# A hand-written issue order of 1190 steps is replaced by another: attention and wave-MLP on one core

## The chip, the cores and the metric

The kernel runs on one core of a Trainium2 chip. The metric is the device time of one execution in microseconds (us), as the median of several runs. The kernel before takes 230.06 us (three runs, 229.84 to 230.63).

The core has a matrix engine TensorE (PE, with its weight load PEld shown apart), VectorE (DVE), ScalarE (ACT), GpSimd (POOL), and SyncE (SP), which here only issues DMAs. PE writes into PSUM, which has eight banks of 128 x 512 float32; the other engines read PSUM and write SBUF.

## The reference

There are two parts, one after the other, for 8 batches of 576 positions:

```python
# attention: q, k, v are (8, 8, 576, 64); factor 4, scale 1/8
q_d, k_d, v_d = means of q, k, v over groups of 4 positions        # 144 positions
out_d  = softmax(scale * q_d @ k_d.T) @ v_d                         # pooled
out_up = np.repeat(out_d, 4, axis=2)
scores = np.where(np.abs(i - j) < 4, scale * q @ k.T, -1e9)         # local band
x = out_up + softmax(scores) @ v                                    # then (8, 576, 512)
# wave-MLP
theta = x @ w_theta
y = einsum('ts,bsd->btd', w_tok_r, x * cos(theta)) + einsum('ts,bsd->btd', w_tok_i, x * sin(theta))
u = x + y
return u + np.maximum(u @ w_ch, 0.0)
```

Inputs and output are float32; the kernel computes in bfloat16 with float32 sums.

## The kernel before

The whole kernel is one list of steps. The string `ORDER` (from L57) holds 1190 words. A word is a kind of step in two letters and a place of one or two characters; the loop at L758 takes the words from left to right and issues the next step of that kind. Steps of one kind come in a fixed sequence (batch by batch, the table `STEPS` at L720), so a word says when the next one comes, not which. The place is, for casts, copies and products, the engine (`a` ACT, `v` DVE, `g` POOL); for steps that write PSUM, one bank or two (`23` is banks 2 and 3); for loads, one of 16 staging slots in SBUF in base 36 (`NSTG`, L44). A function `pin` (L744) ties every instruction to the one issued before it on its engine, so the words set the order on each of the five engines exactly. Between engines only data, banks, buffers and slots make one wait for another.

One batch passes through these kinds:

- Loads on SP: `lk`, `lq` (L287, 288 KB each, four for a batch, two heads each), `lv`, `lw` (L347, two halves of a v tile, 128 KB); weights once: `la` (theta, L240), `lb` (W_tok, nine loads, L253 to L257), `lc` (channel, L240). v of batch 0 comes whole (`l1`, L365). A slot is free again when its cast has read it.
- Casts to bfloat16: `ck`, `cq` (L295, tiles k_tm, q_tm), `cv` (L396), `ca`, `cc` (L243), `cb` (L261).
- `tp` transposes q and k on PE (L302, nine 128x128 matmuls, two banks), `ev` copies the result to kT or qT (L315). For batch 7 a DMA transposes (`dk`, L306) and L312 copies.
- `kd`, `qd`: sums over four positions (on POOL in two products, L329 and L332 or L335; on DVE L321); `pv`, `vd`: those of v (L404, L407; L412).
- Pooled attention: `sd` scores (L426), `ed` exponentials on ACT (L437, tile pd), `nd` product with vd (L447, L452), `xn` division, `xd`, `xc` transposition (L466, L470).
- Local attention in windows of 64: `ps` scores (L482, three units a batch), `ex` exponentials on ACT (L490, tile pm), `mk` the band mask (L503 on POOL, L505), `po` product with v (L515, five chunks), `nm` division on DVE (L523, L524, tile tmp), `xt` transposition (L537), `xa` adds both parts into xT (L545, DVE).
- Wave-MLP: `th` theta (L556, four matmuls of 512 columns, four steps a batch), `cs` cosine and sine on ACT (L561, L562), `tt`, `ct`, `zt`, `zp`, `zc` or the DMA `dz` (L568, L573, L574, L577, L587, L590, L581) the same for the last 64 positions; `xm` transposes x (L595, on PE; for batches 6 and 7 the DMA `dx`, L605), `zz` multiplies (L620, DVE); `mx` mixes the tokens (L636, nine matmuls of 288 columns, eight steps a batch), `ua` adds x (L641, DVE, tile uT).
- Output: `up` and `uc` transpose u on PE (L650, L653) for batches 0 to 3, the DMA `du` (L645) for 4 to 7; `ch` the channel product (L666, four matmuls), `rl` ReLU and sum on DVE (L674, tile osb), `st` the store (L680). `ut`, `dt`, `ht`, `rt`, `ss`, `sr` do the last 64 positions for two batches at a time (L656, L695, L700, L709).
- `wp`, `wc`: W_tok is transposed on PE once (L273) and copied to WT (L278), nine steps, between the first batches.
- `te`, `ts`: an Exp or a Sin of one column on ACT (L770), put ahead so that the table of that function is loaded before it is needed; the compiler puts an ACT_TABLE_LOAD wherever the function's set changes. `wm`: matmuls on zeros (L764), that keep PE at work while the first loads come.

Batches overlap: while the wave-MLP of one is on PE, the scores of the next two are.

The loop itself:

```python
    for word in ORDER.split():
        kind, place = word[:2], word[2:]
...
        if kind in TABLE:

            nc.scalar.activation(out=idle, in_=pihc, func=TABLE[kind])
            pin()
            continue
        STEPS[kind][0](*next(todo[kind]), place)
        pin()
```

Of the kernel before, what the change touches and what calls it, by code (L numbers as in the profile page):

```python
# [57 lines left out]
kcg l10 l11 l12 l13 kcv lk4 lq5 c1a wm7e0 kcg c1g t101 lk6 lk7 ckg c1a ckg c1v t123 e1a kcv e1v wm737 tp01 x12 cqa x13  # L58
lq8 x14 cka x15 cqg evv cva lk9 tp67 ckg cvv cva lqa lqb tp01 lk1 cqg x14 cva wm521 evv evv cqa qdv tp23 cva la3 eva
pv47 vda wm624 ps01 kdg la6 ps23 ex kdv ckg lq4 ex wm656 wm717 lq2 ps01 qdg lk5 sd67 mkv ckv cqg sd45 po23 ed lk8 cag  # L60
ed ex po67 lq9 lba nm cba nd45 nm nd23 xn cag mkg cqa tp01 po67 xn po45 nm lkb eva xd0 mkg ckg lq7 cka xca la1 po23 nm
# [1 line left out]
evv lw th0 th2 lv0 cbv lw zz cbg tt3 xm4 lv3 cs cbg cbv ct cbg cbg cs lvb lw lw wp0 wcv wp1 wcv ztg wp5 th3 wp1 lv8
wcv xm2 cbg xm0 zz zp7 tp45 cs qdg wp3 wp6 zz wcv lw zz wcv wcv zca eva wp7 wcv wp1 wca te wp0 wcv ps34 ps56 ex ex
ps12 mx0 lq1 cvg lk2 lka mx7 lqc mx3 qdv cvg ua lk7 ex ua lk0 mkv mkv kdg sd67 po45 nm sd12 lq4 cva lk5 lk9 cvg cvg ed
ed mx0 ua ua lq3 pv67 po45 po23 nm mx0 vda mkg nd67 lk8 nd45 lkb nm xn xn lq6 ckg ckg tp12 mx3 po45 ua lca ua nm cqg
cqg tp67 eva eva xd0 ckg ckg up1 lq7 po23 lvc xcv nm tp45 xt67 cqg mx0 cqg xt23 eva xt45 lv4 qdg kdg uca lw lv0 lw lw
lv3 lv1 lw lw xa xa tp67 cka ts ckg ckg th1 th2 xa th5 lk8 xm4 evv cs cqg xm1 ckv th3 zz tt4 up6 lq6 lqb cs zz tp12
xm7 ua cs ucv ct cs cqg eva te ztv xm6 zz zz mx0 ua tp34 zp7 tp56 ps12 zcv mx7 mx0 ex cvv kdg evv eva lk7 lk9 cvg lk4
qdg ua up7 uca sd12 mkv ps34 po56 ex ua ccv lcc lc5 kdg nm mkv mx0 sd34 ed po56 cvg cvg ua cqg mx7 nm ua ed mx0 ua lk2  # L70
cka cqg ps67 lqd lq0 cva po45 nm lca ex po23 ckg ckg nm pv01 lvb mx6 vda lk6 utv lw tp45 eva lv1 lw cca ccv nd01 nd23
ua xn xn qdg tp67 mx5 eva lv8 lv9 cqg cqg lw lw ccg ps34 qdg ps67 ua ps12 kdv ex ex xd0 lva xca lw mkg mkg lqc lq0 ch5
rl ckg ckg cvg cvg ch3 sd67 xt45 mkg ed rl ex ts mx0 xa xt67 po45 lv5 th1 cs xa nm ua tp23 th7 up4 up1 ucv xt56 xa mkv
lv4 ch0 eva po56 po23 cvg lq2 tt4 uca th1 cs th7 nm st nm xm2 lqb rl lq1 zz lqd ct cvg xm6 lw cqg ch5 cs zz cs cqa te
up0 up1 rl sd23 ucv po67 ch4 nm rl ch0 rl ucv tp67 lv7 ed cvg pv45 vdv lk8 lk9 eva st st tp23 eva xm0 ztg lk0 lka lw
xm1 zz zz zp7 ch6 zca lvc lv3 kdg nd45 xn nd23 ckg tp01 cva xn qdg utg mx7 cka ps23 rl kdg eva ps01 ua po45 mx6 up7 ex
ex lw lw lv8 nm qdg lw cqg po45 cqg ucv lvb lv2 lw sd23 sd01 lv5 ed mx7 lw lw ua tp23 nm xd4 ed ckg ckg xca st evv
# [730 lines left out]
```

## Time and profile before

| | |
|---|---|
| median of 3 runs | 230.06 us (229.84 to 230.63) |
| span of the profiled execution, first to last instruction | 232.2 us |
| instructions | 9404 |
| PE busy (PEld) | 217.7 us (152.6) |
| DVE, ACT, POOL busy | 187.7, 156.2, 145.0 us |
| mean granted clock of PE | 0.993 |
| share of the 16 DMA engines, main queue | 81.9% |
| read from and written to HBM | 33.98 and 9.44 MB |

The profile is of one execution, whose span is 2.1 us above the median of the timed runs. Its times run from the first instruction. A row of a view names the line of the kernel, the engine, the operation, output and input tiles, and in brackets the idle time of the engine ahead of it with what ended that. A busy PE is one whose matmuls follow each other; matmuls are pipelined, so a row's duration can overlap that of the next.

### The profile page before, as it was taken

What the parts mean: (1) busy time and instruction counts of PE and PEld (TensorE: products, weight loads), DVE (VectorE), ACT (ScalarE), POOL (GpSimd) and SP (SyncE); (2) the same over time, 40 slices, a digit from 0 to 9 for tenths busy, and PEclk for the clock granted to TensorE, in tenths of its full rate; (3) what the DMA queues carried; (4) which work ended last, traced back from release to release, by engine and by line L of the source; (5) the groups of instructions that cost most, each with busy time, mean ns of one, the idle gap of its engine ahead of it and who ended that gap; (6) DMA issues with size and microseconds to landing.
All of it is one profiled execution on the core that took longest, in us unless ns stands there. A gap on an engine that the chain in (4) does not pass through costs nothing.

```text
span 232.2 us, 9404 instructions
## 1 busy us (share of the span) xinstructions
PE 217.7 (94%) x3943; PEld 152.6 (66%) x3970; DVE 187.7 (81%) x367; ACT 156.2 (67%) x243; POOL 145.0 (62%) x192
## 2 busy tenths in 40 slices
...
GB/s 217 395 390 390 291 114 238 361 300 118 265 391 179 165 245 285 243 142 214 205 165 347 307 213 115 206 153 92 67 149 109 71 127 193 138 159 137 142 227 245
DMA packets 76795, 49.41 MB, mean 213 GB/s; under 512 B 61136, under 2 KB 61392, under 8 KB 76752
## 3 DMA queue, kind: packets, MB, share of 16 engines
q1 hardware_dynamic: 76096, 47.76, 81.9%
q10 hardware_dynamic: 656, 1.05, 1.3%
...
HBM read 33.98 MB, written 9.44 MB: 187 GB/s over the span
## 4 chain that ended last, share of the span: by engine, by line
PE 60%; DMA 10%; POOL 10%; issue 6%; ACT 5%; DVE 4%; SPq 4%; DVEq 0%; POOLq 0%; ACTq 0%
PE PS L636 21%; PE PS L666 9%; PE PS L556 8%; DMA st<-in_q_dram 6%; PE PS L302 4%; POOL two L329 3%; PE PS L515 2%; SPq L347 2%; DMA st<-in_k_dram 2%; PE PS L537 2%; DMA ur<-uT 2%; POOL q_tm L295 2%; PE PS L482 2%; PE PS L447 1%; PE PS L595 1%
## 5 line engine op out<-in xcount | busy, mean ns | idle before, releaser
L636 PE MATMUL PS<-WT,z 128*128 128x288 bf16 x576 | 78.0, 287 | 0.0
L636 PEld LDWEIGHTS <-z 128*128 128x128 bf16 x576 | 53.9, 98 | 15.9 <-issue 1.3
L641 DVE TENSOR_TENSOR uT<-PS,xT 128x288 bf16<-128x288 f32 x64 | 28.6, 452 | 12.7 <-PE PS L636 10.9
L561 ACT ACTIVATE cs<-PS,pihc 128x512 bf16<-128x512 f32 x32 | 22.0, 689 | 21.1 <-PE PS L556 13.4
L556 PE MATMUL PS<-wth,xT 128*128 128x512 bf16 x116 | 30.8, 383 | 0.7 <-issue 0.2
L666 PE MATMUL PS<-wch,uT 128*128 128x512 bf16 (+1 forms) x122 | 29.8, 373 | 0.9 <-issue 0.6
L524 DVE TENSOR_TENSOR tmp<-PS,rl 128x512 bf16<-128x512 f32 x40 | 27.7, 692 | 1.4
L545 DVE TENSOR_TENSOR xT<-PS,xdT 128x928 bf16<-128x928 f32 (+1 forms) x24 | 22.3, 952 | 3.7 <-PE PS L537 2.3
L674 DVE SCALAR_TENSOR_TENSOR osb<-PS,ur 128x512 f32<-128x512 f32 x28 | 19.1, 687 | 7.1 <-DMA ur<-uT 3.0
L490 ACT ACTIVATE pm<-PS 128x1024 bf16<-128x1024 f32 (+1 forms) x24 | 20.5, 880 | 6.2 <-PE PS L482 6.1
L577 POOL TENSOR_TENSOR zT<-xT,cst 128x512 bf16<-128x512 bf16 x7 | 9.7, 1383 | 20.6 <-ACT cst L574 20.6
L295 POOL CAST k_tm<-st 128x576 bf16<-128x576 f32 x23 | 15.1, 668 | 11.2 <-DMA st<-in_k_dram 11.1
L396 POOL CAST v_w<-st 128x512 bf16<-128x512 f32 x21 | 13.3, 651 | 10.6 <-DMA st<-in_v_dram 10.5
L770 ACT ACT_TABLE_LOAD x15 | 19.2, 1283 | 0.3
L666 PEld LDWEIGHTS <-uT 128*128 128x128 bf16 x132 | 11.9, 98 | 11.2
L562 ACT ACTIVATE cs<-PS 128x512 bf16<-128x512 f32 x32 | 19.1, 597 | 0.0
L556 PEld LDWEIGHTS <-xT 128*128 128x128 bf16 x128 | 11.7, 99 | 10.6 <-issue 0.6
L295 POOL CAST q_tm<-st 128x576 bf16<-128x576 f32 x23 | 15.4, 686 | 4.9 <-DMA st<-in_q_dram 4.7
L503 POOL TENSOR_TENSOR pm<-pm,band 128x512 bf16<-128x512 bf16 x16 | 18.3, 1164 | 0.0
L329 POOL TENSOR_TENSOR two<-qT 128x576 f32<-128x576 bf16 x14 | 16.5, 1177 | 0.7 <-ACT qT L315 0.4
L620 DVE TENSOR_TENSOR z<-PS,cs 128x1024 bf16<-128x1024 bf16 x24 | 15.8, 684 | 0.5 <-ACT cs L562 0.3
L437 ACT ACTIVATE pd<-PS 128x864 bf16<-128x864 f32 x16 | 13.8, 889 | 2.5 <-PE PS L426 2.5
...
## 6 DMA issues: line engine op xcount, KB each, us to landing
...
```

The costliest lines, as they stand in the source:

```text
L295: COPY[w](out=to, in_=of)
L329: nc.gpsimd.tensor_tensor(out=t, in0=src[:, :, 0:2], in1=src[:, :, 2:4], op=ALU.add)
L490: nc.scalar.activation(out=pm[(3 * b + u) % NPM][:, :, 0:n].rearrange("p e c j w -> p e (c j w)"), in_=at.pop(("ps", b, u))[:, :, 0:4 * W ...
L524: nc.vector.tensor_tensor(out=tmp[(NCH * b + c) % NTMP].rearrange("p g (j d) -> p g j d", d=D), in0=ps[:, :, :, 0:D], in1=r.unsqueeze(3).t ...
L545: nc.vector.tensor_tensor(out=xT[b % 2][:, :, lo:lo + cnt].rearrange("p e (m j) -> p e m j", j=4), in0=at.pop(("xt", b, u))[:, :, 0:cnt].r ...
L556: nc.tensor.matmul(out=ps, lhsT=xT[b % 2][:, dc, P * c:P * c + P], rhs=wth[:, dc, :], start=(dc == 0), stop=(dc == 3))
L561: nc.scalar.activation(out=t[:, 0, :], in_=ps, func=AF.Sin, bias=pihc, scale=1.0)
L562: nc.scalar.activation(out=t[:, 1, :], in_=ps, func=AF.Sin, bias=0.0, scale=1.0)
L636: nc.tensor.matmul(out=ps, lhsT=z[b % 2][:, j, P * dc:P * dc + P], rhs=WT[:, j, cols], start=(j == 0), stop=(j == 8))
L641: nc.vector.tensor_tensor(out=uT[b % 2][:, dc, cols], in0=at.pop(("mx", b, i)), in1=xT[b % 2][:, dc, cols], op=ALU.add)
L666: nc.tensor.matmul(out=ps[:, cols], lhsT=uT[b % 2][:, dc, P * c:P * c + P], rhs=wch[:, dc, cols], start=(dc == 0), stop=(dc == 3))
L770: nc.scalar.activation(out=idle, in_=pihc, func=TABLE[kind])
```

## The change

Only the string `ORDER` changes; no line of code does, nor how many steps of each kind there are. Seen per step, 820 of the 1190 stand in another place of their engine's order, 95 casts, copies, means and products have another engine, and many have other banks or slots. The engines of the places sum up as (before, after): `ck` POOL 23, 20, ACT 7, 9; `cv` POOL 21, 18, ACT 13, 17; `uc` ACT 9, 4, DVE 7, 12; `zt` POOL 7, 5; `cb` ACT 1, 3, POOL 6, 6, DVE 2, 0; `kd`, `qd`, `mk`, `ev`, `cq`, `xc`, `zc`, `cc`, `ut`, `c1` by one to three. The warm-up matmuls at the very start have other banks, and one word `wm010` adds one of 64 columns. The hints `te` and `ts` stand at other places, and in five places more the function's set changes: 21 table loads in place of 16.

Lines of the order around the mask of batch 6 (`sd56 mkv po23` before, `mkv ex sd23 xt01 ed th7 ch5 xa po23` after), and those of the sines of batch 0:

```diff
-up0 uca th4 lvb sd56 mkv po23 lw lw xt01 utg dt ua dk7 cvv nm th7 du ed ts evg nd56 xa nd23 tt0 xn xn ct qdg mkv mkg
-tp67 cag xt45 la0 xt01 nm lb3 lb4 lb5 cqg lbc xa lba lb2 xt23 xa eva tp67 lb8 cqg lb1 caa ts th4 kdg cs cbg xm5 xa lv7
...
+lkc lbd lbe lbf lb0 lq5 xt45 eva cba cag cbg cba nm xa eva lb6 lq2 lv1 ckg lva lbd kdg cag xt67 cbg cbg lw lbb lw tp23
+xa xt01 cba ts th4 cs th6 xm7 cbg cqg evv th5 xa cs tt0 ct wp4 cqv zz wp6 cs wcv th1 wcv ztv xm0 wp6 zz wp7 zp5 wcv
...
+mx5 ex up4 ua mkv ex sd23 xt01 ed th7 ch5 xa po23 th6 nd01 nm tt2 ch3 xn nd01 lv0 st evg dkb mkg lv1 ss st st lve lw
```

ACT ahead of the sines of batch 0. The names: uT are the halves that hold W_tok here, q_tm and k_tm casts of batch 1, kT and qT their transposed copies, xdT the pooled part of x, cs cosine and sine. Before:

```order
L261 CAST uT_111<-st 128x576
L295 CAST q_tm_79<-st 128x9x64
L315 COPY kT_63<-PS 128x2x576
L295 CAST k_tm_74<-st 128x9x64
L470 COPY xdT_99<-PS 128x576
L315 COPY qT_65<-PS 128x1152
L243 CAST wth<-st 128x512
L770 ACT_TABLE_LOAD
L770 ACTIVATE idle<-pihc 128x1
L561 ACTIVATE cs_105<-PS,pihc 128x512
```

After:

```order
L243 CAST wth<-st 128x512
L295 CAST q_tm_79<-st 128x9x64
L295 CAST k_tm_74<-st 128x9x64
L315 COPY kT_63<-PS 128x2x576
L261 CAST uT_111<-st 128x576 x2
L315 COPY qT_65<-PS 128x1152
L261 CAST uT_112<-st 128x576
L770 ACT_TABLE_LOAD
L770 ACTIVATE idle<-pihc 128x1
L561 ACTIVATE cs_105<-PS,pihc 128x512
```

Two more casts of W_tok (L261) stand ahead of the table load, and the copy L470 is gone from ACT; the cast of W_theta (L243) comes first instead of last.

SP around the loads of batches 5 and 6. Before; the two k loads of the row after the ten v loads are of batches 6 and 7, and the eight q loads behind them are all of batch 6's and 7's:

```order
L680 DMA out_dram<-osb_122 128x512
L680 DMA out_dram<-osb_118 128x512
L680 DMA out_dram<-osb_119 128x512
L695 DMA_TRANSPOSE utr<-ut_115 128x4x128
L347 DMA st<-in_v_dram 64x8x64 x10
L287 DMA st<-in_k_dram 128x576 x2
L287 DMA st<-in_q_dram 128x576 x8
L347 DMA st<-in_v_dram 64x8x64
L287 DMA st<-in_k_dram 128x576
```

After; here the q load alone in the third row is batch 6's first, and the next two its second and third:

```order
L287 DMA st<-in_k_dram 128x576
L347 DMA st<-in_v_dram 64x8x64 x3
L287 DMA st<-in_q_dram 128x576
L347 DMA st<-in_v_dram 64x8x64 x3
L287 DMA st<-in_q_dram 128x576 x2
L347 DMA st<-in_v_dram 64x8x64
L680 DMA out_dram<-osb_121 128x512
L287 DMA st<-in_k_dram 128x576 x2
L347 DMA st<-in_v_dram 64x8x64 x2
L287 DMA st<-in_q_dram 128x576
L347 DMA st<-in_v_dram 64x8x64
```

The q loads of batch 6 come among those of k and v of batches 5 and 6 and ahead of three stores (L680) that stood before them.

SP around the transposes of u of batch 4 (ur0<-uT0). z1<-zT is the last part of z of batch 5, osb are stores. Before:

```order
L645 DMA_TRANSPOSE ur0_113<-uT0_111 128x4x128
L680 DMA out_0_dram<-osb4_122 128x512
L581 DMA_TRANSPOSE z1_104<-zT_110 128x4x128
L347 DMA st_126<-in_v_dram 64x8x64 x2
L645 DMA_TRANSPOSE ur0_113<-uT0_111 128x4x128 x2
L347 DMA st_126<-in_v_dram 64x8x64
L680 DMA out_0_dram<-osb0_118 128x512
```

After:

```order
L645 DMA_TRANSPOSE ur0_113<-uT0_111 128x4x128
L680 DMA out_0_dram<-osb3_121 128x512
L709 DMA out_0_dram<-osb2_120 64x512
L680 DMA out_0_dram<-osb4_122 128x512
L645 DMA_TRANSPOSE ur0_113<-uT0_111 128x4x128
L347 DMA st_126<-in_v_dram 64x8x64
L645 DMA_TRANSPOSE ur0_113<-uT0_111 128x4x128 x2
L581 DMA_TRANSPOSE z1_104<-zT_110 128x4x128
```

The last two transposes of ur0, which stood behind z1 and two v loads, now stand ahead of z1, and one v load stands between them and the one before.

More of the change, by code (lines that the diff above doesn't have):

```diff
@@ L57 @@
 ORDER = """
[L58 to L61, printed above, removed]
-tp67 cag xt45 la0 xt01 nm lb3 lb4 lb5 cqg lbc xa lba lb2 xt23 xa eva tp67 lb8 cqg lb1 caa ts th4 kdg cs cbg xm5 xa lv7
@@ L63 @@
[L63 to L77, printed above, removed]
@@ L78 @@
-tp01 eva mx6 mkg xt45 xt23 ua ua cva cvg cvg xt01 cka ts cvg xa xa mx7 th6 xa po45 nm pv23 tt0 th1 lk4 xm4 st st mkg
-th5 vdv st cs nd23 ua zz ct cqg cqg ztg tp67 th4 cs dt po01 cs cs te xn evv po23 mx5 kdg qdg xm4 xm6 mx7 nm ps01 ex nm
-ps23 ua lvd ua ex ch5 ps01 ex qdg zz lw lw xm7 zz rl kdg zp6 zz mkg nd23 xn lv1 lva lv3 mx5 zca sd67 lw ps01 ex po34
-mx2 ua lw ed tp01 sd67 cva nm po34 eva cvv cvg ed lw up5 uca ua mx2 cvg nm cvg lvc xd3 ua pv04 xcv lk7 lk0 mx7 lq9 lq6
-lq2 lqd lq8 lqb lq5 ckg ckg vda lq7 lw xt56 mkv cqg cqg po34 lk4 xt01 xa xa ch2 st cva ts lv6 th5 up6 ckg xm0 nm th1
@@ L93 @@
[L93 to L96 removed]
+wm0e0 l10 c1v l11 lk2 c1g l13 l14 lk5 t101 lq6 lk7 lq8 lq9 c1g cka kcg c1v ckg kcv t123 lk0 e1a tp45 cqg kcg cqg cqg
@@ new lines @@
+wm637 kcv e1v x10 eva cka x13 x12 cvv x14 tp56 cka cva cvv evv lq1 x17 tp01 evv cva cqg cva tp23 la2 lv3 lk5 wm521 lq6
+la4 laa pv67 wm524 eva kdg ps23 lb7 lk0 lq1 lk9 lb8 vda ps01 qdv kdv ps45 wm656 wm617 ex qdg cqg ckg sd23 ex mkv po01
+sd67 ed ckv ed po23 ex nm caa cqa wm010 nm mkg nd67 nd45 xn po23 po01 cka mkg cag xn tp67 xd4 nm nm xcv po23 tp01 lab
+lkc lbd lbe lbf lb0 lq5 xt45 eva cba cag cbg cba nm xa eva lb6 lq2 lv1 ckg lva lbd kdg cag xt67 cbg cbg lw lbb lw tp23
+xa xt01 cba ts th4 cs th6 xm7 cbg cqg evv th5 xa cs tt0 ct wp4 cqv zz wp6 cs wcv th1 wcv ztv xm0 wp6 zz wp7 zp5 wcv
@@ new lines @@
+up6 th7 ucv xt01 up6 ch5 xa cva uca po01 po23 tt4 th6 rl ckv cs cqa nm xm7 th5 ct zz ch4 xm7 nm cqg mkg ckg mkg cvg
+ckg cs up6 rl cs zz sd23 uca po01 ckg ztg cvg qdg cqg up4 ch5 nm ch6 tp01 ucv rl ed rl pv45 lv6 tp23 lw lq3 lkd lw eva
+xm6 zp7 lw lv1 lk2 lw st vdv xm0 lv5 lv0 lq9 lkc ch1 zca zz zz eva nd45 nd67 tp23 xn ps45 xn rl eva ex mx0 ua ps23
+po67 up4 kdg qdg mx5 ckg cqa ex uca nm sd01 po23 ua sd67 mx4 nm ed xd5 cka tp23 ed xcv ua tp01 evv mx6 xt45 ua cqa eva
+cvg kdg xt23 cva cvg cva xa mkg te cvg mkg xa xt01 mx6 xa cqg ckg th7 po45 pv23 tt0 lv7 lw lw nm lq1 lv6 th1 vdv th4
@@ new lines @@
+xm5 lw lv9 lq2 nd23 lq3 lvf st lkd lke cs lw lw cs ct lq8 lva st lkb lk4 lw ua zz th7 tp01 po56 cs xn eva cs po23 nm
+mx4 te mx5 xm7 ps01 qdg qdg ex cvg kdg utg ckg ckg mkg cvg ztv nm ps23 ua ua zz zp5 xm4 zcv zz ex xm6 ch7 nd45 ps23
+mx0 rl xn zz sd45 ex po12 ps67 mx3 ed ex cvg tp45 sd67 cvg cqg nm ua ua ed mkg po23 nm up0 cqg ckg cvv xd1 mx2 pv36
+mx7 xca evv ua xt12 vda ucv xa po34 ts cka xt56 ch0 up1 cvg th2 xa cs ucv cqa nm ua th5 mx1 tp67 th2 ua rl cs lkd lw
+lv0 dt xt01 mkv kdg ckg po45 xa eva tp67 lv9 st st lv2 lqf lw lv3 lw nm cs st lw dk4 lqb st lke lq1 xm3 cqa eva zz
```

35 lines of the change are left out of this document (22 added, 13 removed).

## The prediction

> **What bounds the kernel now.** First the page: busy times and the chain that ended last; then the cores view.
>
> ```profile
> PE 217.7 (94%) x3943; PEld 152.6 (66%) x3970; DVE 187.7 (81%) x367; ACT 156.2 (67%) x243; POOL 145.0 (62%) x192
> PE 60%; DMA 10%; POOL 10%; issue 6%; ACT 5%; DVE 4%; SPq 4%; DVEq 0%; POOLq 0%; ACTq 0%
> ```
>
> ```profile
> core 0: 232.2 us, clock 0.993
> ```
>
> TensorE (PE) is busy in 94% of the span and the change leaves its work as it is, but for one 64-column warm-up matmul. So the time can move only through the 14.5 us in which PE is not busy (232.2 less 217.7), and through the clock of its matmuls. Where they lie shows in the windows view (a stretch, its length, then busy time of PE, PEld, DVE, ACT, POOL, the granted clock, the DMA share, GB/s):
>
> ```profile
> 0.00:10.00 10.00, 8.21 (x48) 4.00 (x49) 5.92 (x28) 4.65 (x6) 6.81 (x27) 1.00 0.81 291
> 10.00:20.00 10.00, 8.84 (x228) 5.88 (x228) 9.47 (x11) 8.82 (x15) 8.85 (x12) 1.00 1.05 393
> 20.00:30.00 10.00, 8.42 (x200) 6.60 (x201) 9.21 (x18) 8.15 (x13) 8.89 (x13) 0.83 1.02 307
> 30.00:40.00 10.00, 9.95 (x204) 8.32 (x204) 8.35 (x18) 9.70 (x16) 8.28 (x11) 1.00 0.73 169
> ...
> 180.00:200.00 20.00, 19.74 (x323) 13.05 (x326) 16.80 (x35) 5.97 (x14) 1.16 (x1) 1.00 0.60 138
> ...
> 220.00:233.00 13.00, 7.86 (x41) 3.79 (x39) 6.75 (x11) 0.40 (x1) 0.00 (x0) 1.00 0.70 213
> ```
>
> The first 30 us hold 1.79 + 1.16 + 1.58 = 4.5 us, and the last 12.2 hold 4.3 (the drain: ReLU sums and stores, with which both orders end alike). What is left, some 5 us, lies in between. The view of waits for PE from 40 to 230 us names it (total, times, longest):
>
> ```profile
> PE PS L515 <- DVE pm L505: 0.8, 1, 0.8
> PE PS L302 <- POOL q_tm L295: 0.8, 1, 0.8
> PE PS L666 <- issue: 0.6, 4, 0.2
> PE PS L482 <- ACT kT L315: 0.6, 1, 0.6
> PE PS L650 <- issue: 0.5, 1, 0.5
> PE PS L515 <- DVE osb L674: 0.4, 1, 0.4
> PE PS L515 <- DVE xT L545: 0.3, 1, 0.3
> PE PS L426 <- POOL qd L335: 0.3, 1, 0.3
> PE PS L700 <- issue: 0.2, 1, 0.2
> ```
>
> The rows sum to 4.5 us, and that is what another order can win between the start and the drain. It can also make new rows of this kind, and no engine need be full for that.
>
> **Edits with one answer.** By the place letters of the words, VectorE (DVE) has nine small operations more (five of them `uc` copies from ACT), ACT one more, GpSimd (POOL) ten fewer. At 0.45 to 0.69 us (the mean of the DVE groups of L641 and L620, the nearest in size) that is 4 to 6 us more for an engine that is idle for 44 us of the span: at nothing, as long as no such operation stands directly ahead of one that PE waits for; those that do are priced as waits below. The warm-up matmul goes at nothing: it stands among the idle time of 20 to 30 us.
>
> **Loads of batch 6: −1.1 us.** POOL and PE rows of the timeline:
>
> ```profile
> 126.13 1.40 POOL L295 CAST q_tm<-st 128x576 bf16<-128x576 f32 x2 [1.00 <-DMA st<-in_q_dram]
> ...
> 134.20 0.66 POOL L295 CAST k_tm<-st 128x576 bf16<-128x576 f32 x1 [3.83 <-DMA st<-in_k_dram]
> ```
>
> ```profile
> 135.53 0.68 PE L302 MATMUL PS<-ident,q_tm 128*128 128x128 bf16 x9 [0.81 <-POOL q_tm L295]
> ```
>
> POOL stood still for 1.00 and 3.83 us because q and k of batches 6 and 7 came late; the cast that followed held PE 0.81 us, and the mean after it another 0.27 (row of waits, 0.3). In the changed order the SyncE queue issues the first q load of batch 6 some 16 DMAs earlier in relation to the rest and no longer keeps ten v loads and eight q loads in a block. Sixteen loads of 288 KB at the 393 GB/s of the row 10:20 (the most that a row shows) are 12 us, against the 1.00 and 3.83 by which the casts were late. Both waits go: −1.1, with 0 and −1.6 as ends (the upper one includes the 0.5 of L650, which ends in the same stretch). I put that 0.5 at −0.3, since its releaser isn't shown.
>
> **Transposes of u, batch 4: −0.7.** DVE's row there:
>
> ```profile
> 178.04 1.29 DVE L674 SCALAR_TENSOR_TENSOR osb<-PS,ur 128x512 f32<-128x512 f32 x2 [2.11 <-DMA ur<-uT]
> ```
>
> DVE waited 2.11 us for a DMA transpose, and PE then 0.4 and 0.3 us (rows L515 <- osb, <- xT). The changed SP order issues the three transposes ahead of that of z, with one unit of PE work more between them and L674. Ends −0.7 and 0; I take −0.7, since two small waits need only 0.7 of cover.
>
> **Mask of batch 6: −0.8.**
>
> ```profile
> 151.10 2.18 POOL L312 COPY kT<-st 128x1152 bf16<-128x1152 bf16 x1 [2.58 <-DMA st<-k_tm]
> ...
> 151.94 1.88 DVE L505 TENSOR_TENSOR pm<-pm,band 128x1024 bf16<-128x1024 bf16 x1
> ...
> 153.88 0.32 PE L515 MATMUL PS<-v_w,pm 64*64 64x65 bf16 x16 [0.83 <-DVE pm L505]
> ```
>
> The mask product on DVE took 1.88 us here beside a POOL copy of 2.18, and PE waited 0.83. The words there were `sd56 mkv po23`, with nothing for PE between the mask and its reader but the 12 matmuls of `sd`. Now they are `mkv ex sd23 xt01 ed th7 ch5 xa po23`: a theta step (`th`) and a channel product (`ch`), eight matmuls of 512 columns, stand between.
>
> ```profile
> L556 PE MATMUL PS<-wth,xT 128*128 128x512 bf16 x116 | 30.8, 383 | 0.7 <-issue 0.2
> ```
>
> 30.8 / 116 = 0.27 us each, 2.1 for eight, so the 0.83 goes even if the product stays as slow; ends −0.8 and 0.
>
> **The copy of k that holds a bank (L482 <- ACT kT, 0.6): −0.6.** Before, the banks `01` of a transposition were asked for again by scores (`ps01`) right behind the copy that empties them (`eva`); now a mixing step stands between the copy and `ps23`.
>
> ```profile
> L636 PE MATMUL PS<-WT,z 128*128 128x288 bf16 x576 | 78.0, 287 | 0.0
> ```
>
> Nine of its matmuls at 78.0 / 576 = 0.135 are 1.2 us, more than the wait; ends −0.6 and 0.
>
> **New waits: +1.5.** Six places of the new order have a PE step that takes a bank, or a tile, whose last reader stands just ahead on another engine: the v means of batch 1 (`pv23`, whose bank a `nm` on DVE still reads), the first channel product of batch 1 (behind sines of batch 2 on ACT), a transposition of k of batch 6, the second pooled product of batch 5, a mixing step of batch 3 (behind a `nm`), an `xt` of batch 6. Rows of the kind above are 0.2 to 0.4 us for one, so 6 × 0.25 = 1.5; ends 0 and 6 × 0.4 = 2.4. Loads of `w_ch` and v of batch 2 wait on SP for a slot which a POOL cast frees, with everything on SP behind them: +0.2, ends 0 and 1.0 (POOL's wait above, 1.00).
>
> **Start: +0.5.** Rows of ACT, POOL, PE and SP:
>
> ```profile
> 20.30 0.69 ACT L261 CAST uT<-st 128x576 bf16<-128x576 f32 x1
> ...
> 25.09 1.12 ACT L315 COPY qT<-PS 128x1152 bf16<-128x1152 bf16 x1 [1.09 <-PE PS L302]
> 26.74 1.28 ACT L770 ACT_TABLE_LOAD   x1
> ```
>
> ```profile
> 29.43 6.68 SPq L347 DMA_DIRECT2D st<-in_v_dram  x6
> ...
> 32.05 1.15 POOL L577 TENSOR_TENSOR zT<-xT,cst 128x512 bf16<-128x512 bf16 x1 [0.34 <-ACT cst L574]
> ...
> 33.15 0.66 POOL L261 CAST uT<-st 128x576 bf16<-128x576 f32 x1
> ...
> 34.40 1.76 PE L273 MATMUL PS<-ident,uT 128*128 128x128 bf16 x30
> ...
> 36.89 3.48 PE L636 MATMUL PS<-WT,z 128*128 128x288 bf16 x27
> ```
>
> ACT gets two more casts of W_tok ahead of the sines, 2 × 0.69 = 1.38 us, and loses the copy of x's pooled part; it stood still 1.09 us for PE in this stretch, which takes most of that up: 0. But the last two W_tok loads now stand behind v loads. Every step from the last load to the first mixing matmul follows without a hole: cast 33.15 to 33.81, transposes from 34.40, mixing at 36.89. Four v halves of 128 KB at 393 GB/s are 0.33 us each, so 1.3 later by bytes. The slack between cast and transposes is 0.6; and the product zT, 1.15 us directly ahead of the last cast on POOL, is now DVE's, which lets the cast start earlier, when its data are there. 1.3 − 0.6 = 0.7 at the most by bytes; I take 0.5. By issue it is worse: the v rows of SP took 6.68 us for six, 1.1 each, and three now stand ahead: 3.3 − 0.6 = 2.7 (the first rival). On the other side PE's 1.58 us of idle time in 20 to 30 could shrink, by 0.4 at a guess from the ACT row's 1.09. Ends −0.4 and +2.7.
>
> **Table loads: 0.** In the new order the hints `te` and `ts` stand in places where five more loads result.
>
> ```profile
> L770 ACT ACT_TABLE_LOAD x15 | 19.2, 1283 | 0.3
> ```
>
> Five × 1.28 = 6.4 us more for ACT. Four lie in two pairs, Exp then Sin, ahead of the last sines of batches 6 and 7, where ACT is busy 5.97 us of 20 (row 180:200) and PE has a mixing step and more between; the fifth stands among the last stores. Six others come right ahead of the operation that needs them instead of at a hint, where ACT has less idle time, but they don't wait for PE themselves. At nothing; if the cover is gone at one place, 1.28.
>
> The Trainium skill (ScalarE: Activation LUTs, What ACT_TABLE_LOAD costs) gives about 2.66 us for a switch, a drain of 1380 ns included: by it the pair would take 5.3 us rather than 2.6 and the cover would not hold, +1 to +2.7. The row speaks against it: behind the load at 26.74, the dummy activation stands at 28.04, 1.30 later, with no drain between.
>
> **Sum.** −1.1 −0.3 −0.7 −0.8 −0.6 +1.5 +0.2 +0.5 = −1.3 us. The profiled execution's span is 232.2, 2.1 above the median of the runs (230.06); the difference is the same for both, so a span of 230.9 and a median of **228.8 us**. With two or three terms at their worse or better ends, not all one way, this case has 227.9 to 229.8.
>
> **Rivals.**
> *The last W_tok loads decide (slower).* If three v loads ahead on SP cost their 1.1 us each, the first mixing step comes 2.7 later instead of 0.5: 228.8 + 2.2 = 231.0. It decides from the point where the last cast of W_tok ends more than 0.6 us later than now. For it: SP's row, and POOL's waits for DMA in this stretch; after it PE has 9.95 of 10 us busy (30:40), so nothing pays the loss back. Against it: DMA, not SP, may have set those 1.1 us, and then bytes count. Chance 0.24.
> *The waits only move (same).* New bank waits of 0.4 rather than 0.25 (+0.9) and no gain at the copy of k (+0.6) make −1.3 + 0.9 + 0.6 = +0.2: 230.3. For it: PE is so full that each new hole counts. Chance 0.20.
> *Most of the 4.5 us goes (faster).* −4.5 of old waits, +1.0 of new, start at nothing, +0.2: 226.8. Chance 0.08.
> *The clock.* In the row 20:30 PE had 0.83 of its clock, and these matmuls took twice their time:
>
> ```profile
> 24.37 0.68 PE L302 MATMUL PS<-ident,q_tm 128*128 128x128 bf16 x9
> ...
> 26.26 1.12 PE L302 MATMUL PS<-ident,k_tm 128*128 128x128 bf16 x9
> ```
>
> 0.17 × 10 = 1.7 us of clock are lost there. The longest gap of PE in the 5 us ahead:
>
> ```profile
> 22.91 0.42 PE L466 MATMUL PS<-ident,xdn 72*128 72x72 bf16 x8 [0.70 <-ACT kT L315]
> ```
>
> Those gaps change with the order, so the stretch may go (−1.7: 227.1) or another may come (+1.7: 230.5). Chance 0.03 each: one such stretch in 232 us is all that this trace shows, and both orders keep PE about as busy. The Trainium skill (TensorE: Matmul & The Clock Gate, Part 1) ties the half clock to an idle window of about 3.4 us; the trace's longest gap ahead of its one stretch is 0.70 us, so by that rule the stretch would not be here, and no row shows what sets it off.
>
> **How the numbers follow.** The forecast has 0.42, of which 0.36 is below 229.37 and 0.06 above; the first rival 0.24 (slower); the second 0.20 (0.13 same, 0.07 slower); the third 0.08 (faster); the clock 0.03 faster and 0.03 same. 0.3% (0.7 us) is about what a measurement of this kernel tells from no change. So faster 0.47, same 0.22, slower 0.31. The range goes from the third rival to a little over the first, 226.9 to 231.6; outside lie a start worse than 2.7 and several terms that all fall one way.
>
> **What would show it.** Right: no POOL wait for q or k of batch 6 over 1 us, no PE row L302 <- POOL of 0.8; no L515 <- pm of 0.8; first L636 within 0.5 us of 36.89; PE waits from 40 to 230 at 3 us. Wrong: L636 first at 38 or later with L273 waiting for a cast; a sum of PE waits of 4.5 or more; PEclk below 1 in a second place; an L561 row behind two table loads ahead of an idle PE.

## The result, and the profile after

The changed kernel takes **239.77 us** (median of 4 runs, 238.01 to 241.08), the kernel before 229.95 (4 runs, 229.67 to 230.63). The ratio is 1.041, with a 95% interval of 1.037 to 1.045: slower by 9.8 us, where 228.8 and a gain of 1.3 were forecast.

The profiled execution of after has a span of 237.3 us, and that same run took 239.02, which is its span and 1.7. The kernel before was profiled once more, unchanged, beside the experiments (the run b_same below): span 227.3, run 228.97, again 1.7 apart. So the execution on which the prediction rests, with its span of 232.2, must have taken about 233.9, not "2.1 above the median" but 3.8. It was an unusually long one. From here on, after is compared with b_same. Its run lies 1.2 below the median of its ten (230.17), after's 0.75 below the median of its four, so both are rather short executions, and a wait that b_same lacks may be there in another.

Page of after, busy times and the chain that ended last:

```profile
PE 220.5 (93%) x3971; PEld 152.3 (64%) x3971; DVE 191.7 (81%) x375; ACT 162.9 (69%) x249; POOL 135.0 (57%) x181
PE 73%; DMA 13%; DVE 5%; issue 3%; ACT 2%; POOL 1%; SPq 0%; DVEq 0%; POOLq 0%
```

DMA has 13% of the chain, which the page puts down to loads of k and W_tok at the start. Where the time went shows first in the start of the same mixing step (L636) in both traces. The first step of batch 0 starts 4.2 us later than in b_same. At the last step of batch 1 the delay is 4.6, at the first of batch 2 it is 7.9, at the first of batch 3 7.7, at the fifth of batch 3 9.6, and at the last step of all 9.8. So there are three places: the start (+4.2), 80 to 100 us (+3.3) and 124 to 141 us (+1.9). The last two are not all loss, because the new order also puts other steps of PE between the same mixing steps: at the first step of batch 6 the delay is back at 8.05, and from there to the end it grows to 9.8 with no idle PE in either trace. What was lost must be read from PE's idle time. The windows view of after shows the first two places in the PE column:

```profile
20.00:30.00 10.00, 7.45 (x248) 5.71 (x244) 9.16 (x20) 8.57 (x13) 9.92 (x13) 1.00 1.05 317
30.00:40.00 10.00, 8.47 (x160) 6.41 (x163) 8.53 (x16) 7.87 (x15) 5.25 (x9) 1.00 0.94 157
...
80.00:100.00 20.00, 17.54 (x307) 11.46 (x293) 15.54 (x30) 16.19 (x25) 15.06 (x18) 1.00 1.05 246
```

The same rows of b_same:

```profile
20.00:30.00 10.00, 8.30 (x217) 6.18 (x218) 9.79 (x20) 9.25 (x15) 9.31 (x13) 1.00 1.05 303
30.00:40.00 10.00, 9.95 (x229) 8.32 (x230) 8.68 (x18) 9.41 (x16) 8.03 (x11) 1.00 0.77 158
...
80.00:100.00 20.00, 19.79 (x391) 14.44 (x391) 18.00 (x36) 17.76 (x26) 19.61 (x26) 1.00 1.04 253
```

**The start.** POOL's timeline in after has the last two casts of W_tok, each waiting for its load:

```profile
35.05 0.67 POOL L261 CAST uT<-st 128x576 bf16<-128x576 f32 x1 [3.12 <-DMA st<-in_moe_w_tok_i_dram]
36.63 0.67 POOL L261 CAST uT<-st 128x576 bf16<-128x576 f32 x1 [0.92 <-DMA st<-in_moe_w_tok_i_dram]
```

PE's timeline in after: the transposes of these tiles, and the first mixing step.

```profile
37.36 0.23 PE L273 MATMUL PS<-ident,uT 128*128 128x128 bf16 x1 [1.36 <-POOL uT L261]
...
40.36 1.89 PE L636 MATMUL PS<-WT,z 128*128 128x288 bf16 x14
```

In b_same the last cast of W_tok starts at 32.66 and the first mixing step here:

```profile
36.15 1.03 PE L636 MATMUL PS<-WT,z 128*128 128x288 bf16 x7
```

**The middle.** PE's waits in after from 40 us on, the whole list:

```profile
PE PS L636 <- issue: 1.4, 1, 1.4
PE PS L650 <- issue: 1.1, 1, 1.1
PE PS L568 <- issue: 1.0, 1, 1.0
PE PS L636 <- DVE tmp L524: 0.4, 1, 0.4
PE PS L404 <- DVE uT L641: 0.3, 1, 0.3
PE PS L302 <- ACT qT L315: 0.2, 1, 0.2
```

PE's waits in b_same from 40 us on, the whole list:

```profile
PE PS L666 <- issue: 0.6, 4, 0.2
PE PS L515 <- DVE xT L545: 0.3, 1, 0.3
PE PS L515 <- DVE osb L674: 0.2, 1, 0.2
PE PS L700 <- issue: 0.2, 1, 0.2
```

These two lists answer to the nine rows and 4.5 us that the prediction set out to win. In b_same the sum is 1.3, and 0.8 of that are gaps of 0.16 us, the room of one matmul whose record is missing (3943 matmuls against 3970 weight loads); the prediction's 4.5 holds the same 0.8. What another order could win here was 0.5 us in this execution, and at most 1.7 in one of median length, if the 1.2 that it is longer were all such waits. And after has three waits of over 1 us in which PE waited for nothing that the profile shows. Two of them, in PE's timeline:

```profile
80.08 1.03 PE L636 MATMUL PS<-WT,z 128*128 128x288 bf16 x7
82.48 0.41 PE L636 MATMUL PS<-WT,z 128*128 128x288 bf16 x2 [1.37 <-issue]
...
87.70 0.20 PE L568 MATMUL PS<-xT,wth 128*128 128x64 bf16 x1
88.95 0.60 PE L568 MATMUL PS<-xT,wth 128*128 128x64 bf16 x15 [1.05 <-issue]
```

PE stops between the seventh and the eighth of nine matmuls that read the same tile z and sum into the same bank, and between the first and the second of sixteen that read the same xT. No data, bank or semaphore changes between them. So what was late was the instruction itself.

### The profile page after: what moved, and what is told of

The parts are those of the page before. It is cut to its first block, busy times and chain, and to the rows that moved or that the text cites. A ratio compares the mean times of both kernels' runs of the same rounds, so it can differ in the third digit from the quotient of the medians.

```text
span 237.3 us, 9418 instructions
## 1 busy us (share of the span) xinstructions
PE 220.5 (93%) x3971; PEld 152.3 (64%) x3971; DVE 191.7 (81%) x375; ACT 162.9 (69%) x249; POOL 135.0 (57%) x181
## 4 chain that ended last, share of the span: by engine, by line
PE 73%; DMA 13%; DVE 5%; issue 3%; ACT 2%; POOL 1%; SPq 0%; DVEq 0%; POOLq 0%
PE PS L636 29%; PE PS L666 10%; PE PS L556 8%; DMA st<-in_k_dram 7%; PE PS L302 5%; DMA st<-in_moe_w_tok_i_dram 3%; DMA st<-in_moe_w_tok_r_dram 3%; PE PS L482 3%; PE PS L537 2%; PE PS L515 2%; PE PS L650 2%; PE PS L447 2%; PE PS L595 2%; PE PS L568 2%; PE PS L700 1%
## 5 line engine op out<-in xcount | busy, mean ns | idle before, releaser
L636 PE MATMUL PS<-WT,z 128*128 128x288 bf16 x576 | 78.3, 286 | 1.8 <-issue 1.4
L636 PEld LDWEIGHTS <-z 128*128 128x128 bf16 x576 | 53.9, 98 | 18.1 <-issue 3.2
L556 PE MATMUL PS<-wth,xT 128*128 128x512 bf16 x128 | 32.4, 380 | 0.1
L666 PE MATMUL PS<-wch,uT 128*128 128x512 bf16 (+1 forms) x132 | 31.4, 373 | 0.0
L577 POOL TENSOR_TENSOR zT<-xT,cst 128x512 bf16<-128x512 bf16 x5 | 5.8, 1157 | 31.1 <-ACT cst L574 30.9
L329 POOL TENSOR_TENSOR two<-kT 128x580 f32<-128x580 bf16 x14 | 16.6, 1182 | 9.0 <-ACT kT L315 8.9
L329 POOL TENSOR_TENSOR two<-qT 128x576 f32<-128x576 bf16 x13 | 15.1, 1164 | 10.2 <-ACT qT L315 7.8
L295 POOL CAST q_tm<-st 128x576 bf16<-128x576 f32 x21 | 13.9, 666 | 6.4 <-DMA st<-in_q_dram 6.4
L556 PEld LDWEIGHTS <-xT 128*128 128x128 bf16 x128 | 11.1, 98 | 9.9 <-DVE xT L545 1.0
L503 POOL TENSOR_TENSOR pm<-pm,band 128x512 bf16<-128x512 bf16 x14 | 16.3, 1188 | 0.0
L315 ACT COPY qT<-PS 128x1152 bf16<-128x1152 bf16 x10 | 11.3, 1127 | 6.3 <-PE PS L302 6.3
```

The lines of the kernel that those rows point to most:

```text
L329: nc.gpsimd.tensor_tensor(out=t, in0=src[:, :, 0:2], in1=src[:, :, 2:4], op=ALU.add)
L503: EW[w].tensor_tensor(out=t[:, x], in0=t[:, x], in1=m[:, x], op=ALU.mult)
L556: nc.tensor.matmul(out=ps, lhsT=xT[b % 2][:, dc, P * c:P * c + P], rhs=wth[:, dc, :], start=(dc == 0), stop=(dc == 3))
L636: nc.tensor.matmul(out=ps, lhsT=z[b % 2][:, j, P * dc:P * dc + P], rhs=WT[:, j, cols], start=(j == 0), stop=(j == 8))
L666: nc.tensor.matmul(out=ps[:, cols], lhsT=uT[b % 2][:, dc, P * c:P * c + P], rhs=wch[:, dc, cols], start=(dc == 0), stop=(dc == 3))
```

## The experiments

Two theories stood at the outset. **Loads (start):** the last W_tok loads stand behind v loads on SP's queue, POOL stands still at their casts, and PE follows (the prediction's first rival). **Refill (F), in the middle:** PE's instructions are themselves brought by DMA. The page of after has a queue for that:

```profile
q8 instruction: 31, 0.51, 1.1%
```

(its columns are packets, megabytes and share of the 16 engines' time). That is 31 packets of 16 KB, and PE's 3971 matmuls and 3971 weight loads are 7942 instructions, 256 for a packet. The Trainium skill (Trainium Architecture — The Big Picture, The software stack) has an instruction at 64 bytes, which makes 256 of them in 16 KB; the trace agrees. The packets are spread over the whole span, from 16.8 to 222.9 us. The three waits of after stand ahead of PE's instructions 3002, 3258 and 4794, counted with the weight loads: each is 186 more than a multiple of 256. The packets that belong to them start at 79.92, 86.40 and 124.19 and take 1.07, 1.21 and 1.41 us; PE goes on at 82.48, 88.95 and 127.04, some 1.4 us after each packet's end. The rivals to it: a wait that the trace doesn't record (a bank, a semaphore), and the clock, which was 1.00 in these stretches.

### Whose start, whose middle: a_bstart and b_astart

Each kernel has one order up to the first mixing step and the rest of the other; ten banks and slots had to be moved in the one and twelve in the other where they meet.

```diff
 a_bstart
-<after's words up to the first mx>
+<before's words up to the first mx>
 b_astart
-<before's words up to the first mx>
+<after's words up to the first mx>
```

> The changed order with the start undone: up to the first mixing step of batch 0 the words of before, from there those of after (ten slots and banks moved to free ones). In the profiles the first mixing step starts 3.5 us later after the change (36.89 before, 40.36 after). Theory S (the start is most of the loss): the whole loss is 9.8 us, and over half of it goes, 230.5 to 234 us. Theory F (the start is 2 to 4 us of it, and the rest is TensorE waiting in the middle at places where its own instructions have not been fetched): 235 to 238 us, first mixing step at 36 to 38, and rows of PE with 'issue' of about 1 us each stay between 75 and 130 us.

> The mirror image: up to the first mixing step the words of after, from there those of before (twelve slots and banks moved). Theory S: over half of the 9.8 us, 235 to 240 us. Theory F: 232 to 234.5 us, first mixing step about 3.5 us later than in the order of before. If start and rest add up, this run's loss and that of the mirror image sum to 9.8 us.

a_bstart took 238.96 us (ratio 1.039, 1.032 to 1.047), b_astart 234.73 (1.021, 1.015 to 1.028). With after's start, before loses 2.1%. In its profile the delay against b_same is 5.3 us at the first mixing step, 6.9 at the last of batch 1 (one wait of 1.1 behind the splice is part of it) and 6.6 at the end, with no long wait by `issue` in the middle; so those waits belong to after's middle. The opposite kernel doesn't undo the start: its first mixing step is at 38.88, not at 36, and it has new waits of 1.8 us (for exponentials on ACT, ahead of that step) and 1.6 (for divisions, in two), where after has 0.4 for divisions. It still shows `issue` waits of 1.1 and 1.4 us in the middle, at the same two lines as after's first two. The splice spoils the sum of the two parts; only the places can be read from it.

### Moving the instructions against the packets: a_shift112 and b_shift32

Warm-up matmuls of 512 columns at the very start are replaced by more of 64 columns. They stand where PE waits for the first loads, and each later instruction of PE moves on by 112 places (after) or 32 (before).

```diff
 a_shift112
-wm0e0 l10 c1v l11 ...
+wm001 wm001 ... (70 of them) l10 c1v l11 ...
 b_shift32
-c1a wm7e0 kcg ...
+c1a wm7a0 wm701 wm701 ... (20 of them) kcg ...
```

> The changed order with the 14 warm-up matmuls of 512 columns at the very start replaced by 70 of 64 columns: about the same PE time there (0.8 us more at most, where PE waits for the first loads), but every later instruction of PE stands 112 places further in its stream. No step moves. In the changed profile PE's three 'issue' waits (1.37, 1.05 and 1.13 us) stand at its instructions number 3002, 3258 and 4794, all 186 in a block of 256. Theory F: waits of this kind stay at 186 in a block of 256 and so stand at other steps; with the blocks cut at these other places I expect 1.2 us of them in place of 3.6, and 1 to 3 us off the time (237 to 239). Rival (the three waits belong to their steps: a bank, a semaphore, a buffer): they stay at the same three steps and the time stays within 1 us of 239.8 or rises by the 0.8.

> The order of before, where 4 of its 14 warm-up matmuls of 512 columns at the very start are replaced by 20 of 64 columns: about the same PE time (0.3 us more at most), and every later instruction of PE stands 32 places further. No step moves. Theory F: before, the cuts between blocks of 256 fall at steps where PE is slow enough; 32 places further they fall at dense stretches of 64x64 matmuls, and by the durations in its profile I expect some 4 to 7 us more waiting with 'issue' as the cause, 233 to 237 us. Rival (the place of an instruction in the stream is nothing to the time): 230.0 to 230.8 us.

PE's waits in a_shift112 (four lines were added above the code, so L640 is L636 of after and L470 its L466):

```profile
PE PS L541 <- issue: 2.4, 1, 2.4
PE PS L470 <- issue: 1.7, 1, 1.7
...
PE PS L640 <- issue: 0.6, 1, 0.6
```

And in b_shift32, where b_same had none over 0.3 (one line more than in before):

```profile
PE PS L303 <- issue: 1.1, 1, 1.1
...
PE PS L538 <- issue: 1.0, 2, 0.6
```

The waits left their old places and stand at other steps, ahead of PE's instructions 956, 2490 and 3002 (a smaller one of 0.2 at 700) in the one, and 1980, 3004 and 5048 in the other. With after's three, that makes ten instructions of seven different lines, and each is 184 to 188 more than a multiple of 256; if place had nothing to do with it, five values of 256 would hold one in 51. Data and banks are as before, so a bank or semaphore that the trace lacks is out. The expected smaller sum did not come: the waits sum to 4.7 us where after has 3.55. Yet a_shift112 took 237.91 (1.032, 1.021 to 1.042), 1.9 less than after; its runs reach from 235.9 to 239.8, so this says little. b_shift32's runs scatter from 230.9 to 239.1 us, so no ratio is given; its place is evidence, its time is not.

### The kernel before again: b_same

No edit.

> The kernel before, unchanged. Its timed runs elsewhere have spans of 226.4 to 229.8 us, but the execution whose profile the prediction was made from has 232.2. Theory: that profile was a slow draw of the same waits (a half-clock stretch of 1.7 us, two 'issue' waits of 0.65 and 0.50, loads that came late at 135 us), and this profile shows a span of 227 to 230 with less of them. Rival: a profile is always some 3 us longer than a timed run, and this one shows 232 again.

It took 230.17 us (0.999, 0.995 to 1.003). Its waits stand above. Its packets come as in after, 31 of them; it isn't free of refills, but they come in time.

### Less for the DMA queues to do: a_lessdma

From batch 3 on, q and k loads bring half the columns. The order is after's, word for word.

```diff
+            half = b >= 3 and int(w, 36) in whole
+            cols = slice(0, S // 2 if half else S)
-            nc.sync.dma_start(out=t, in_=src[...])
+            nc.sync.dma_start(out=t[:, cols], in_=src[...][:, cols])
```

> The changed order; from batch 3 on the loads of q and k bring only half of each row (288 of 576 columns, the rest of the slot is stale), so that the DMA engines have some 6 MB less to move. No instruction of PE moves. Theory F (PE's instruction blocks come late because their DMA packets stand behind data): the three 'issue' waits at 82, 89 and 127 us (3.6 us) shrink to below 1 in sum, and 2.5 us or more come off (237 or less, with POOL's waits for loads gone as well). Rival (the fetch takes as long with idle DMA engines): the three waits stay as they are.

It took 234.99 us (two runs; 1.018, 1.009 to 1.026), 4.8 less than after, with the same PE stream. Windows of after around the two waits (the last columns are the clock, the DMA share and GB/s):

```profile
80.00:84.00 4.00, 2.63 (x81) 1.63 (x67) 2.50 (x4) 2.88 (x5) 2.91 (x4) 1.00 1.11 239
84.00:88.00 4.00, 3.90 (x76) 2.29 (x75) 2.85 (x6) 3.60 (x6) 3.65 (x4) 1.00 1.10 245
88.00:92.00 4.00, 3.05 (x31) 1.75 (x31) 2.44 (x7) 3.52 (x8) 3.42 (x5) 1.00 0.99 256
```

And of a_lessdma:

```profile
80.00:84.00 4.00, 3.45 (x74) 2.18 (x72) 3.44 (x6) 3.46 (x7) 4.00 (x5) 1.00 0.76 203
84.00:88.00 4.00, 3.95 (x83) 2.37 (x83) 2.78 (x5) 4.00 (x8) 3.25 (x5) 1.00 0.76 215
88.00:92.00 4.00, 3.92 (x53) 2.42 (x53) 3.73 (x8) 3.98 (x7) 3.65 (x5) 1.00 0.63 140
```

The one `issue` wait over 0.3 us that is left is 0.39, again ahead of instruction 3002. With less on the queues the packets start sooner: 2.2, 1.8 and 0.5 us after PE has crossed into the block ahead of theirs, where in after it was 3.2, 3.9 and 2.8. Against after's profile 0.7 us is won at the first mixing step, 2.9 by the first of batch 2, and 3.7 from the fifth of batch 3 to the end. The 0.7 come ahead of the first halved load, which is issued at 41 us, and so are a difference between two executions. The 2.9 behind them answer to the 3.2 by which the refill waits shrank. The result doesn't hang on one execution: eight profiles of this section and the next have after's middle and whole loads (after, a_bstart, a_wtok, a_first, a_both, a_both_nowm, a_start, a_hints), and in them the waits at these three places sum to between 1.9 and 4.4 us; in the three with halved loads they sum to 0.39, 0 and 0. That other loads also come sooner stays a second effect that these runs can't take apart.

### The loads of the start: a_wtok, b_wtok, a_first, a_both

a_wtok takes only the last two W_tok loads ahead of the v loads in after (one q load gets another slot for it). b_wtok does the reverse to before: three v halves go ahead of its second-last W_tok load, and one more ahead of the last.

```diff
 a_wtok
-lb6 lq2 lv1 ckg lva lbd kdg cag xt67 cbg cbg lw lbb lw tp23
+lb6 lq2 lbd lb1 lv9 ckg lva kdg cag xt67 cbg cbg lw lw tp23
 b_wtok
-tp67 lb8 cqg lb1 caa ts th4 kdg cs cbg xm5 xa lv7 evv lw th0 th2 lv0
+tp67 lvd lve lvf lb8 cqg lw lb1 caa ts th4 kdg cs cbg xm5 xa evv th0 th2
```

> The changed order with one thing undone: the last two loads of W_tok are issued ahead of the v loads again (three slots moved). In the changed profile PE waits 1.36 us at 37.36 for the last cast of W_tok, and the first mixing step is at 40.36. Theory S2 (the first rival of the prediction): that wait goes to below 0.3, the first mixing step starts 1.0 to 1.5 us earlier, and 1.0 to 1.5 come off 239.8. Rival: another wait takes its place ahead of the first mixing step (the sines on ACT, the copies of W_tok on DVE), no change within 0.5 us.

> The order of before with one thing of the change: three v loads of batch 1 stand ahead of the second-last load of W_tok, and the second half of one ahead of the last (three slots moved to free ones). Theory S2: PE waits for the last cast of W_tok ahead of the first mixing step, 0.7 to 2.2 us, 231 to 232.5 us. Rival (by bytes the loads come 1.3 us later, and the slack of 0.6 and what PE has to do otherwise take it up): under 0.5 us, 230 to 230.6.

a_wtok took 236.77 us (1.027, 1.020 to 1.034), 3.0 less than after, more than the 1.0 to 1.5 expected; POOL's casts wait 0.67 and 0.64 in place of 3.12 and 0.92, PE's wait at L273 is gone, and the first mixing step starts 2.2 earlier. Its refill waits are also 1.1 smaller. POOL's timeline, and PE's:

```profile
31.62 0.67 POOL L261 CAST uT<-st 128x576 bf16<-128x576 f32 x1 [0.67 <-DMA st<-in_moe_w_tok_i_dram]
32.94 0.67 POOL L261 CAST uT<-st 128x576 bf16<-128x576 f32 x1 [0.64 <-DMA st<-in_moe_w_tok_i_dram]
```

```profile
38.17 2.01 PE L636 MATMUL PS<-WT,z 128*128 128x288 bf16 x15
```

b_wtok took 234.33 (1.018, 1.012 to 1.025): that one edit costs before 3.8 us. Its POOL and PE rows show the way from the load to PE:

```profile
34.10 0.67 POOL L261 CAST uT<-st 128x576 bf16<-128x576 f32 x1 [3.64 <-DMA st<-in_moe_w_tok_i_dram]
34.73 1.15 POOL L577 TENSOR_TENSOR zT<-xT,cst 128x512 bf16<-128x512 bf16 x1
```

```profile
35.94 0.40 PE L587 MATMUL PS<-ident,zT 128*128 128x128 bf16 x4 [2.33 <-POOL zT L577]
...
39.17 1.03 PE L636 MATMUL PS<-WT,z 128*128 128x288 bf16 x7
```

The cast that waits isn't what PE wants next; the product zT is, and it stands behind the cast on POOL. Moved loads both ways, and the time follows both ways: the loads theory holds. It is not the whole of the start, since a_wtok's first mixing step is still 2.0 us later than b_same's. Differences of 1 us at this step mean little by themselves: with the same words up to there, it starts at 39.63, 40.36 and 42.47 in a_lessdma, after and a_hints, the last with a stretch at half the clock just ahead.

a_first brings the first v tiles of batch 0 ahead of the first k load, for PE's wait of 1.26 us at L376, 9 us into the span. a_both joins it with a_wtok.

```diff
-wm0e0 l10 c1v l11 lk2 c1g l13 l14 lk5
+wm0e0 l10 c1v l11 l13 l14 lk2 c1g lk5
```

> The changed order with one thing undone at its very start: the four loads of v of batch 0 come first again, ahead of the first load of k (which moves two places back). In the changed profile the second group of transpositions of v waits 1.26 us for its cast at 9.32, and everything behind it is 2.1 us late up to 25 us. Theory S1: the wait goes to below 0.5, the first scores come at 16 to 16.5 instead of 17.33, and 0.5 to 1.3 us come off 239.8. Rival: the k load that is late instead takes the same time (first transposition of k at 10.3 or later), no change within 0.5 us.

> The changed order with both parts of the start undone: the four loads of v of batch 0 first, the last two loads of W_tok ahead of v of batch 1. Alone, in profiles, the first brought the first mixing step 0.88 us forward, the second 2.20. Theory S (two separate causes): 3 us forward, at about 37.3 instead of 40.36, and 235 to 237 us as the 'issue' waits stay. Rival (one hides the other): no earlier than 38.2, 236.5 or more.

a_first took 239.75 us (1.034, 1.025 to 1.044), the same as after. The wait is gone, but the k cast is now later and PE waits for that:

```profile
9.28 0.68 PE L302 MATMUL PS<-ident,k_tm 128*128 128x128 bf16 x9 [1.04 <-POOL k_tm L295]
```

The first mixing step came 0.9 earlier in its trace, and the gain was lost to an `issue` wait of 2.5 at 82.8 and a stretch at half the clock. a_both took 237.28 (1.030, 1.024 to 1.036), no better than a_wtok alone; the first mixing step is at 37.79, and the `issue` waits at 3002 and 3258 are 1.8 and 1.6, where a_wtok has 0.9 and 0.5. What is gained ahead of these refills seems to be given back at them.

### Both causes together: a_both_lessdma

a_both with the halved loads.

> The same, and from batch 3 on the q and k loads bring only half of each row (the rest of the slot is stale), which took the 'issue' waits of the changed order from 3.55 to 0.39 us. If start and instruction fetch are the two causes and add up: the span is 237.3 - 3.1 - 3.2 = 231, a time of 232 to 233.5, and what is left over the 230.2 of before is the small new waits, 2 to 3 us. If they share a cause, 234 or more.

233.67 us (1.015, 1.010 to 1.020). No `issue` wait over 0.3 is left, and the first mixing step is at 38.92. So 3.2 us over the 230.5 of before remain with both edits (with halved loads, before itself might be faster, so the rest may be more). Its profile has one stretch of 3.41 us at half the clock, at most 1.7 of these.

### What else the start holds: a_both_nowm, a_start, a_start_lessdma

PE waits a little at many places of after's start: `wm010` for a division on DVE (L764 <- DVE tmp, 0.6), then 0.5, 0.5 and 0.4. The theories (N and N2) are that these waits hold the rest of the start. a_both_nowm is a_both without that word. a_start also puts a cast of k behind the two divisions on DVE, and a_start_lessdma halves its loads.

```diff
 a_both_nowm
-ex nm caa cqa wm010 nm mkg
+ex nm caa cqa nm mkg
 a_start
-sd67 ed ckv ed po23 ex nm caa cqa wm010 nm mkg
+sd67 ed ed po23 ex nm caa cqa nm ckv mkg
```

> Both parts of the start undone as before, and without the one warm-up matmul of 64 columns that the change adds (its bank is one that a division on DVE still reads; PE waits 0.65 us for it in the changed profile, 0.8 and 1.6 in later ones). The prediction put this matmul at nothing. Theory N (the matmul is the wait): 0.4 to 1.5 us off the 237.3 of the run with both undone. Rival (what PE does next waits as long): no change within 0.5 us, and the wait shows at L447 or L515 instead.

> The same, and the cast of k of batch 1 that stands on DVE ahead of the first two divisions of batch 0, and waits there 0.55 us for its load, is issued behind them. Theory N2 (a cast that waits for a load holds DVE's queue, and PE behind it): the waits for DVE's tmp at 21 to 26 us (0.8 + 0.5 + 0.4) go to below 0.6 in sum, the first mixing step comes 0.5 to 1.5 us earlier than with both undone (37.79), 235 to 236.5 us. Rival (the W_tok loads still set the first mixing step): it stays at 37.5 to 38.

> The same with half of each q and k row from batch 3 on (the rest of the slot is stale), so without the waits for instructions. With both undone and less DMA the time was 233.7. If the causes add up, 1 us off that: 232 to 233, and what is left over the 230.5 of before is waits of 0.2 to 0.5 us on DVE and ACT between 40 and 230 us, 1 to 2 us in all.

238.32 us (1.035, 1.028 to 1.042), 236.19 (1.028, 1.020 to 1.037) and 233.78 (1.018, 1.013 to 1.022). Leaving out `wm010` gains nothing; the wait turns up at the next steps, here two rows of PE's list of a_both_nowm up to 40 us:

```profile
PE PS L515 <- DVE tmp L524: 0.7, 2, 0.4
PE PS L447 <- ACT pd L437: 0.5, 1, 0.5
```

Nor does the later cast of k bring the first mixing step forward in the profiles: it is at 38.95 in a_start, 38.83 in a_both_nowm and 37.79 in a_both. But the first two have a stretch at half the clock from 26 us on, up to 1.7 us of this, and a_both has none. By its time a_start lies in its expected range, 1.1 below a_both, with runs from 235.3 to 238.0; with halved loads that gain is gone (233.78 against 233.67). So a gain by either edit isn't shown, and which of the start's small waits decides stays open.

### The table loads: a_hints

The last three `te` hints are taken out, and with them five table loads: 16, as in before.

```diff
-dx ch3 te cs dxe ... mx7 ct te cs ua ... ht7 ch2 te sta
+dx ch3 cs dxe ... mx7 ct cs ua ... ht7 ch2 sta
```

> The changed order without the last three hints for the Exp table, so that ACT has 16 table loads instead of 21 (6.4 us of ACT less in the last 60 us). The prediction put these at nothing: within 1 us of 239.8, no change of the distance between the mixing steps of batches 6 and 7. Rival (they hold the last sines, and so the mixing steps): 1 to 2.7 us off, and the mixing steps from (6,6) on, which lost 1.7 us in the changed profile, move forward.

239.08 us (1.037, 1.025 to 1.049), within after's own range. ACT's busy time from 180 to 210 us falls from 17.88 in after to 13.46 (the fourth number behind the window; PE's is the first), in a_hints:

```profile
180.00:210.00 30.00, 29.73 (x418) 19.76 (x422) 23.13 (x47) 13.46 (x24) 2.31 (x2) 1.00 0.52 113
```

and the mixing steps of batches 6 and 7 follow each other at the same distances in both (21.83 us from the first of batch 6 to the last of all). So five loads of 1.28 cost nothing, as forecast. The 1 to 2.7 us that the prediction worked out from the Trainium skill (ScalarE: Activation LUTs, What ACT_TABLE_LOAD costs) did not show.

## Why the prediction was wrong

**The gains (−1.1, −0.3, −0.7, −0.8, −0.6).** The waits they count are gone in after past 40 us, as predicted: no L302 <- POOL, L515 <- pm or L482 <- ACT kT. But four of the five are gone from b_same too, with not a word changed. They were waits of one long execution: late loads, a slow mask product, a held bank and a refill. Of the 3.5 us only the transposes of u, batch 4, recur (0.3 and 0.2 in b_same), and these 0.5 were in fact won. The step that failed is the one that took an execution 3.8 us above the median as the account of what an order can win, and carried "the difference is the same for both" across.

**The start, +0.5.** It cost 4.2. This is the first rival's mechanism, and its point of decision: the last cast of W_tok starts at 36.63, 4.0 later than in b_same, far beyond the slack of 0.6, and the sign that the prediction set for being wrong came: L636 first at 40.36, with L273 waiting for a cast. The forecast chose the price by bytes; the rival's price by issue, 2.7, was nearer, and the same kind of edit in before costs 3.8 (b_wtok). What both missed is that a waiting cast stops POOL, with zT, the means of q and the rest behind it. The rest, up to 2 us, are small waits for DVE and ACT. The prediction put the moved operations at nothing, DVE being idle for 44 us of the span, unless one stands directly ahead of a step of PE, and it counted no such place in the start.

**`issue`, −0.3 with its releaser "not shown".** This was the row to ask about. It stood at L650, ahead of instruction 4792, 184 more than a multiple of 256. The prediction saw a small wait that would go; in after such waits are 3.5 us. No rival had it.

**New waits, +1.5.** Right in kind and too high: past 40 us there are three such rows, L636 <- DVE tmp 0.4, L404 0.3 and L302 0.2, 0.9 in all, and of the six places only the transposition of k of batch 6 (L302) is surely among them: the other two are in batch 4 and ahead of a bank that the sum into uT frees.

**Loads on SP that wait for a slot (+0.2), table loads (0), the extra warm-up matmul (0).** Right for the table loads and the matmul, by a_hints and a_both_nowm. The +0.2 shows in no row of its own.

**The clock, 0.03 each way.** Too low. Before's long execution had one stretch (its rows show 0.68 and 1.12 us for nine matmuls, not twice the time), but the mean clock was 0.994 or more in 43 of 44 timed runs of before, and 1.000, 0.990, 0.983 and 0.990 in those of after. One stretch of 3.41 us at half the clock is 1.7 us or 0.0075 of a mean over 230 us, so by that reckoning after's runs have none, one, two and one. The median of after then holds about 1.7 us of it. But the runs' times don't follow their clocks (239.02 at 1.000, 238.01 at 0.990), so this share isn't shown. What sets a stretch off wasn't found.

**The sum, as far as it is shown.** Of the 9.8 us between the two profiles' last mixing steps, 4.2 come ahead of the first; a_wtok gets back 2.2 of these. Behind it, after's waits sum to 4.4, of which 3.55 are refills, and b_same's, without the missing records, to 0.5: 3.9 more. These 8.1 are accounted for, and 1.7 are not. That the refills are late because the DMA queues are full rests on the three kernels with halved loads. None of the kernels tried beats before.
